# Attention feeding a mixture of experts on one core: two pairs of heads handled as one unit, with the tail keys in 64x64 quarters of the array

## The chip, the cores and the metric

The kernel runs on one core of a Trainium2 chip. The metric is the device time of one execution in microseconds (us), the median of several executions. The engines of the core are named as in the profile: PE is TensorE (matmuls), PEld its weight loads, DVE is VectorE, ACT is ScalarE, POOL is GpSimd, and SP is SyncE, which here only issues transfers (DMAs). Each engine runs its own instructions in order and waits for others by semaphores.

## The reference

An attention with a soft cap on the scores feeds a mixture of experts in which each token goes to one expert.

```python
batch, n_heads, seq, head_dim = (8, 12, 448, 64)            # cap = 30
scores = q @ k.T / sqrt(head_dim)
scores = cap * tanh(scores / cap)
attn = exp(scores - scores.max(-1)); attn /= attn.sum(-1) + 1e-9
x = (attn @ v) as [3584 tokens, 768]                        # 12 heads x 64
logits = x @ w_gate + modality_bias[modality_id]            # 8 experts
e_idx, gate_w = argmax(logits), softmax(logits)[e_idx]
out[token] = gate_w * (relu(x[token] @ w1[e]) @ w2[e])      # F = 1024
```

## The kernel before, in words

**Two phases.** `attention` works on 48 pairs of heads (six per batch, eight batches; a pair is heads 2p and 2p+1 of one batch). Then `run_slots` works on blocks of 384 tokens of one expert (slots): `ffn1` (tokens times w1), `ffn2` (times w2). In slot 0 some work that is left over from attention is put between the matmuls of `ffn1` by hooks.

**Scores.** The scores of a pair stand as [keys, queries]. The raw keys and queries of a pair (tile `raw`, 128 partitions: 64 dimensions of the one head, 64 of the other) are split by `prep` into two float32r halves, `ah` (high) and `al` (low); a product is three float32r matmuls (high x high, low x high, high x low). A head has 448 keys: three steps of 128 keys (`scores` with step 0, 1, 2) and 64 keys that are left, the tail. In steps 0 to 2 the two heads' matmuls are two at a time, in the upper and the lower 64 rows of the array, each into a bank of a `sc` tile. In step 3 the tails of both heads are one matmul of 128 rows: the 128 tail keys stand in a block with zeros beside them, so that each key meets its own head only.

**Weights.** ACT makes Tanh (`th`) and Exp (`pt`, or `sh` for step 3) from each `sc` tile. There are two `sc` buffers; a Tanh sets its buffer free.

**Sums over keys.** `weigh_own` multiplies the exponentials with `va` (the values) in plain float32, six matmuls, the two heads side by side in the two halves of the array's columns; `weigh_shared` adds the tails with one matmul of 128 rows and 128 columns. The result `xT` [dimension, query] is copied to SBUF by DVE (L603). DVE also adds the three exponential tiles of a head (`add`, L472 and L473, into `tot`).

**Denominators and gate logits.** `sums` works on three pairs at a time: each pair has 32 columns of the array and the same 32 partitions of the bank `glog`; four float32 matmuls per pair accumulate two sums of exponentials and 16 gate logits. `by_token` transposes the result to tokens (`lt`), `logits` divides, `rows_out` transposes `xT` to token rows (four transposes into `tp`) and multiplies by the reciprocal (`xs`), `store` writes them to DRAM.

**Order.** The order on PE is written out by hand (instructions are pinned), over g = 0 to 48, four steps each; the weighing of pair g-1 stands between the scores of pair g. After the last pair of a batch `route` finds each token's expert, in stages; its second PE piece is the small matmul pair `rank`. When seven batches are routed, `early_slot` names the expert of slot 0, whose w1 is loaded and split (`split_w`) and whose tokens are gathered while attention ends; `transpose` turns the gathered rows into `x`.

**Slot 0.** `run_slot` splits `W2_EARLY` of the eight w2 tiles on POOL ahead of `ffn1`, the other tiles behind it, and then loads the next slot's w1:

```python
if n == TW:
    self.load_w2(cur[0], raws, range(W2_EARLY if between else FC), self.nc.gpsimd if between else None)
self.ffn1(n, between)
if between:
    self.load_w2(cur[0], raws, range(W2_EARLY, FC))
    nxt = ahead()
```

The loads of w1 and w2 share four `raw` buffers. In `ffn2` ACT takes each finished half tile out of PSUM (`ot<-py`, two `py` buffers).

## Time and profile before

| | us |
|---|---|
| median of 3 runs (lowest, highest) | 939.42 (939.24, 940.53) |
| the profiled execution, its own time | 939.73 |
| its span, from the first to the last instruction | 938.1 |

The profiled execution spent 1.6 us outside its span. In rows of the trace, a start is counted from the beginning of the span; a busy time of a matmul includes the drain of the array, so that consecutive matmuls overlap, and what a matmul costs in a stream is the distance from its start to the next start. A plain float32 matmul is recorded as two (`x12` for six of them).

### The profile page before, as it was taken

What the parts mean: (1) busy time and instruction counts of PE and PEld (TensorE: products, weight loads), DVE (VectorE), ACT (ScalarE), POOL (GpSimd) and SP (SyncE); (2) the same over time, 40 slices, a digit from 0 to 9 for tenths busy, and PEclk for the clock granted to TensorE, in tenths of its full rate; (3) what the DMA queues carried; (4) which work ended last, traced back from release to release, by engine and by line L of the source; (5) the groups of instructions that cost most, each with busy time, mean ns of one, the idle gap of its engine ahead of it and who ended that gap; (6) DMA issues with size and microseconds to landing.
All of it is one profiled execution on the core that took longest, in us unless ns stands there. A gap on an engine that the chain in (4) does not pass through costs nothing. (4 is left out here: it accounts for less than half of the span.)

```text
span 938.1 us, 14512 instructions
## 1 busy us (share of the span) xinstructions
PE 902.5 (96%) x5360; PEld 699.3 (75%) x5360; DVE 545.9 (58%) x939; ACT 557.6 (59%) x758; POOL 138.8 (15%) x147
## 2 busy tenths in 40 slices
PE   7999999999999998989899999999999999999997
PEld 3444545554545554469899999999999999998997
DVE  4667777778787777567444443433434444427762
ACT  5998888888888886732434444343424444435551
POOL 2000202020202022124310202020201102020000
PEclk8999999999999999999999999999999999999997
DMA  4333434444534533642764735353554646247660
GB/s 143 111 104 120 125 127 127 126 110 144 127 127 103 151 108 93 233 141 71 264 225 129 235 125 201 116 178 129 168 203 146 225 130 206 93 133 258 197 211 7
DMA packets 47467, 140.01 MB, mean 149 GB/s; under 512 B 8687, under 2 KB 9631, under 8 KB 47377
## 3 DMA queue, kind: packets, MB, share of 16 engines
q1 hardware_dynamic: 38464, 106.47, 36.9%
q0 software_dynamic: 8768, 32.42, 10.0%
q8 instruction: 47, 0.77, 0.3%
q14 instruction: 44, 0.35, 0.1%
q10 hardware_dynamic: 144, 0.00, 0.0%
HBM read 117.35 MB, written 22.69 MB: 149 GB/s over the span
## 5 line engine op out<-in xcount | busy, mean ns | idle before, releaser
L460 ACT ACTIVATE th<-sc,isc 128x896 f32<-128x896 f32 x192 | 168.6, 907 | 53.4 <-PE sc L458 53.2
L775 PE MATMUL ph<-x,al 128*128 128x384 f32 (+2 forms) x528 | 167.8, 318 | 0.0
L800 PE MATMUL py<-bh,hh 128*128 128x384 f32 x464 | 159.5, 344 | 5.6 <-ACT ot L805 4.1
L800 PE MATMUL py<-bh,hl 128*128 128x384 f32 x464 | 157.2, 339 | 0.0
L800 PE MATMUL py<-bl,hh 128*128 128x384 f32 x464 | 156.8, 339 | 0.0
L462 ACT ACTIVATE pt<-th,cabs 128x896 f32<-128x896 f32 x144 | 149.5, 1044 | 3.1 <-DVE tot L473 0.4
L771 PE MATMUL ph<-x,ah 128*128 128x384 f32 x384 | 129.8, 338 | 4.7 <-DVE x L754 4.4
L467 PE MATMUL xT<-pt,va 128*64 128x448 f32 x576 | 122.8, 563 | 8.7 <-DVE xT L603 7.1
L772 PE MATMUL ph<-x,ah 128*128 128x384 f32 x384 | 129.2, 336 | 0.0
L727 DVE TENSOR_TENSOR bl<-raw,bh 128x768 fp32r<-128x768 f32 x85 | 78.6, 955 | 52.1 <-ACT bh L726 49.6
L726 ACT CAST bh<-raw 128x768 fp32r<-128x768 f32 x88 | 70.2, 840 | 63.0 <-DMA raw<-in_w_dram 52.6
L775 PEld LDWEIGHTS ph<-x,al 128*128 128x128 f32 x528 | 102.0, 193 | 0.0
L458 PEld LDWEIGHTS sc<-ah 64*128 64x128 f32 (+1 forms) x336 | 36.5, 187 | 77.8 <-ACT pt L462 28.5
L781 ACT ACTIVATE hh<-ph 128x384 fp32r<-128x384 f32 x64 | 30.6, 489 | 105.6 <-PE ph L775 98.4
L805 ACT ACTIVATE ot<-py,mt 128x384 f32<-128x384 f32 x58 | 33.6, 581 | 99.2 <-issue 50.1
L800 PEld LDWEIGHTS py<-bh,hh 128*128 128x128 f32 x464 | 87.5, 189 | 6.5 <-ACT ot L805 4.4
L810 POOL DMA_INDIRECT out_dram<-ot,mt x29 | 33.0, 1137 | 391.0 <-ACT ot L805 310.4
L467 PEld LDWEIGHTS xT<-pt,va 128*64 128x64 f32 x576 | 38.1, 139 | 70.6 <-issue 46.5
L458 PE MATMUL sc<-ah 64*128 64x448 f32 (+1 forms) x336 | 86.8, 445 | 3.0 <-ACT th L460 2.0
L727 DVE TENSOR_TENSOR al<-raw,ah 128x1024 fp32r<-128x1024 f32 x64 | 76.4, 1222 | 22.1 <-ACT ah L726 21.9
L800 PEld LDWEIGHTS py<-bl,hh 128*128 128x128 f32 x464 | 87.6, 189 | 0.3 <-DVE bl L727 0.2
L800 PEld LDWEIGHTS py<-bh,hl 128*128 128x128 f32 x464 | 87.6, 189 | 0.1
(165 smaller groups left out, 1352.3 us busy)
## 6 DMA issues: line engine op xcount, KB each, us to landing
raw<-in_w_dram SPq DMA_DIRECT2D x88, 384.0 KB
raw<-in_w_dram SPq DMA_DIRECT2D x64, 512.0 KB
raw<-in_kq_dram SPq DMA_DIRECT2D x47, 480.0 KB
va<-in_v_dram SPq DMA_DIRECT2D x48, 256.0 KB
xd<-xs POOLq DMA_DIRECT2D x15, 672.0 KB
kq<-in_w_dram SPq DMA_DIRECT2D x2, 512.0 KB
xd<-xs SPq DMA_DIRECT2D x1, 672.0 KB
mapd<-pay,pos POOLq DMA_INDIRECT x32
```

The lines of the kernel that those rows point to most:

```text
L458: pin(pe.matmul(sc[:, j, :S], k[rows, ks], q[rows, KC2:], start=i == 0, stop=i == 2))
L460: nc.scalar.activation(th[:, :n], sc[:, :n, :S], AF.Tanh, scale=self.isc)
L462: nc.scalar.activation(dst, th[:, :n] if step < KU else th[:, 0], AF.Exp, scale=self.cabs)
L467: pin(pe.matmul(xT[j * D : (j + 1) * D, :S], va[:, u * D : (u + 1) * D], pt[:, u], start=u < 2, stop=False))
L726: keep((self.nc.vector.tensor_copy if busy else self.nc.scalar.copy)(hi, raw))
L727: (keep if minus is None else (lambda inst: inst))((minus or self.nc.vector).tensor_tensor(lo, raw, hi, op=ALU.subtract))
L771: nc.tensor.matmul(ph[:, :w], hi[:, fs], self.x[:, k, 0, :w], start=first, stop=False)
L772: nc.tensor.matmul(ph[:, :w], hi[:, fs], self.x[:, k, 1, :w], start=False, stop=False)
L775: nc.tensor.matmul(ph[:, :w], lo[:, fs], self.x[:, k, 0, :w], start=False, stop=last)
L800: nc.tensor.matmul(py[:, :HALF], self.h[a][:, f, rows], self.w2s[f][c][:, cs], start=i == 0, stop=i == 3 * FC - 1,)
L805: nc.scalar.mul(ot[:, cs], py[:, :HALF], mt[:, t, 1:2])
L810: nc.gpsimd.indirect_dma_start(self.out, bass.IndirectOffsetOnAxis(ap=mt.bitcast(I32)[:, t, 0:1], axis=0), ot, None, bounds_check=NT - 1, ...
```

## The change

Two pairs of heads (the even pair A = 2d and the odd pair G = 2d+1 of the same batch) form one unit d, 24 in all.

- **Tail keys.** No zeros are loaded any more: `raw` has 384 own keys, 448 queries and 64 tail keys per head. The tail scores are taken from `raw` itself, in plain float32: four matmuls of 64 rows and 64 columns (`scores_left`), pair by columns, head by rows. One Tanh and one Exp of 896 columns per unit replace two of each of 448 columns. `prep` splits 832 columns in place of 960. The tails' part of the weighing is again four float32 matmuls in quarters (`weigh_left`), pair by rows, head by columns.
- **Copies and rows.** `xT` is two banks wide and copied once per unit; the rows of both pairs are transposed eight at a time into an `sc` buffer and multiplied by one instruction (L561). The store has 256 columns per unit in place of 384 per three pairs.
- **Sums.** Four groups of 32 columns per unit, two matmuls each; transposition, reciprocal and logits once per unit.
- **Order.** Written out anew, by units. The first w1 tiles go into the ring of key and query buffers as these come free; two of the six tiles are cast and subtracted on POOL. `W2_EARLY` is 4 in place of 3.

The core of the diff:

```diff
-W2_EARLY = 3
+W2_EARLY = 4
-            def scores(step, pt, sh, hi, lo):
...
-                n = 2 if step < KU else 1
...
-                        rows = slice(j * D, (j + 1) * D) if step < KU else slice(0, 128)
-                        pin(pe.matmul(sc[:, j, :S], k[rows, ks], q[rows, KC2:], start=i == 0, stop=i == 2))
+            def scores_left(d):
+                shs[d] = xp.tile([128, 2, S], F32, name="sh", bufs=2)
+                sc = ps_s.tile([128, 2, 512], F32, name="sc")
+                for i in range(2):
+                    raw = ring[(2 * d + i) % RING]
+                    for j in range(2):
+                        rows = slice(j * D, (j + 1) * D)
+                        pin(pe.matmul(
+                            sc[i * KR : (i + 1) * KR, j, :S], raw[rows, QL:QK], raw[rows, OWN:QL], start=True, stop=True
+                        ))
+                weights(shs[d], sc)
-            def weigh_shared(xT, sh, va):
-                pin(pe.matmul(xT[:, :S], va[:, 2 * KU * D :], sh, start=False, stop=True))
+            def weigh_left(xT, d):
+                for i in range(2):
+                    rows = slice(i * KR, (i + 1) * KR)
+                    for j in range(2):
+                        o = (2 * KU + j) * D
+                        pin(pe.matmul(
+                            xT[j * D : (j + 1) * D, i, :S], vas[2 * d + i][rows, o : o + D], shs[d][rows, j],
+                            start=False, stop=True,
+                        ))
+                xs_ = kept[d] = xp.tile([128, 2, S], F32, name="xT", bufs=2)
+                pin(V.tensor_copy(xs_, xT[:, :, :S]))
...
-                for t in range(HB):
-                    xs_, tot, sh = kept[h * HB + t]
-                    w = self.pick[:, part] if part < 3 else self.wgt[:, (h * HB + t) % NP]
-                    rhs = (tot[:, 0], tot[:, 1], sh, xs_)[part]
-                    pin(pe.matmul(self.glog[t * GW : (t + 1) * GW, :S], w, rhs, start=part == 0, stop=part == 3))
+                group = lambda x: glog[x * GW : (x + 1) * GW, :S]
+                for i in range(2):
+                    for j in range(2):
+                        pin(pe.matmul(group(2 * i + j), self.pick[:, 0], tots[2 * d + i][:, j], start=True, stop=False))
+                for j in range(2):
+                    pin(pe.matmul(group(j), self.pick[:, 1], shs[d][:, j], start=False, stop=True))
+                for i in range(2):
+                    pin(pe.matmul(
+                        group(2 + i), self.wgt[:, (2 * d + i) % NP], kept[d][:, i], start=False, stop=True
+                    ))
+            for d in range(ND):
+                A, G = 2 * d, 2 * d + 1
+                early, end = d == SOON + 2, d == ND - 1
...
+                scores(A, 0)
+                scores(A, 1)
...
+                if d:
+                    xT = ps_x.tile([128, 2, 512], F32, name="xT")
+                    weigh_own(xT, A - 2)
+                    add(A - 2)
...
+                prep(A + 2)
...
+                scores(A, 2)
+                scores(G, 0)
...
+                if d:
+                    weigh_own(xT, A - 1)
+                    add(A - 1)
...
+                prep(A + 3)
...
+                scores(G, 1)
+                scores(G, 2)
+                if not end:
+                    scores_left(d)
...
+                if d:
+                    weigh_left(xT, d - 1)
...
+                go_on()
+                if d >= 2:
+                    if not early:
+                        logits(d - 2)
+                    tokens(d - 2, nc.sync if early else nc.gpsimd)
...
+                if d:
+                    sums(d - 1)
+                    copy_sums()
```

The first place is PE in the middle of attention. Before, one pair reads, from its weighing (`xT<-pt,va`) on: the sums of three pairs (`glog`), step 2, step 3 (the tails: one matmul in place of two), the transposes of an older pair and the tails' weighing.

```order
L467 MATMUL xT<-pt,va 64x448 x6
L486 MATMUL glog<-tot,pick 32x448 x6
L458 MATMUL sc<-ah_157 128x448 x2
L458 MATMUL sc<-ah_157,al_158 128x448 x2
L458 MATMUL sc<-al_158,ah_157 128x448 x2
L458 MATMUL sc<-ah_157 128x448
L458 MATMUL sc<-ah_157,al_158 128x448
L458 MATMUL sc<-al_158,ah_157 128x448
L516 MATMUL tp<-ident,xT 112x128 x4
L476 MATMUL xT<-sh,va 128x448
```

After the change, the end of a unit on PE: step 2 of the odd pair, then the tails of both pairs and everything that is done once per unit, up to the first scores of the next unit.

```order
L461 MATMUL sc<-ah_158 128x448 x2
L461 MATMUL sc<-ah_158,al_159 128x448 x2
L461 MATMUL sc<-al_159,ah_158 128x448 x2
L472 MATMUL sc<-raw 64x448 x4
L490 MATMUL xT<-sh,va 64x448 x4
L525 MATMUL lt<-ident,gl 112x128 x4
L553 MATMUL tp<-ident,xT 112x128 x8
L509 MATMUL glog<-tot,pick 32x448 x4
L511 MATMUL glog<-sh,pick 32x448 x2
L513 MATMUL glog<-xT,wgt 32x448 x2
L461 MATMUL sc<-ah_152 128x448 x2
```

The tails' scores and everything behind them, up to the next unit's scores, now stand in one run at the unit's end. Before, scores stood between them.

The second place is ACT in slot 0, behind `ffn1`: the casts of the last w2 tiles (`bh`), those of the next slot's w1 (`ah`), and the emptying of the finished `py` tiles (`ot`). Before:

```order
L726 CAST bh_4429<-raw 128x768
L726 CAST bh_4431<-raw 128x768
L726 CAST bh_4433<-raw 128x768
L726 CAST bh_4435<-raw 128x768
L726 CAST bh_4437<-raw 128x768
L726 CAST ah_149<-raw 128x1024
L805 ACTIVATE ot<-py,mt 128x384 x2
```

And after the change:

```order
L770 CAST bh_4320<-raw 128x768
L770 CAST bh_4322<-raw 128x768
L770 CAST bh_4324<-raw 128x768
L770 CAST bh_4326<-raw 128x768
L849 ACTIVATE ot<-py,mt 128x384
L770 CAST ah_148<-raw 128x1024
L770 CAST ah_150<-raw 128x1024
L849 ACTIVATE ot<-py,mt 128x384
```

Four w2 tiles are cast here in place of five, and the first `ot` stands ahead of the next slot's first w1 cast.

## Rows read from the trace of the kernel before

**Rows 1.** The page: the span, and the busy time of each engine with its share and its instructions.

```profile
span 938.1 us, 14512 instructions
PE 902.5 (96%) x5360; PEld 699.3 (75%) x5360; DVE 545.9 (58%) x939; ACT 557.6 (59%) x758; POOL 138.8 (15%) x147
```

**Rows 2.** Busy time by stretch: the stretch and its length, then busy time (and instructions) of PE, PEld, DVE, ACT and POOL, the granted clock as a share, the DMA share and GB/s. The first stretch is the middle of attention; the second goes from the first scores after the seventh batch to the first matmul of `ffn1`; the third is `ffn1` of slot 0, the fourth the beginning of its `ffn2`.

```profile
100.00:150.00 50.00, 49.30 (x309) 25.50 (x309) 38.21 (x73) 43.62 (x52) 7.44 (x8) 1.00 0.42 119
...
358.17:404.84 46.67, 37.19 (x216) 18.64 (x216) 34.64 (x73) 33.37 (x42) 10.28 (x10) 0.96 0.59 176
404.84:438.73 33.89, 33.77 (x200) 30.16 (x200) 21.38 (x88) 5.87 (x11) 11.91 (x11) 0.95 0.30 88
438.73:459.00 20.27, 16.18 (x85) 15.32 (x85) 10.34 (x11) 10.73 (x15) 11.06 (x13) 0.92 0.78 259
```

**Rows 3.** PE in order of time in the middle of attention: start, busy time, line, operation, tiles, array rows*columns, shape, count. One pair goes from 205.04 to 213.30.

```profile
205.04 2.48 PE L467 MATMUL xT<-pt,va 128*64 128x448 f32 x12
207.44 1.70 PE L486 MATMUL glog<-tot,pick 128*32 128x448 f32 x12
209.08 0.47 PE L458 MATMUL sc<-ah 64*128 64x448 f32 x2
...
209.89 0.47 PE L458 MATMUL sc<-ah 128*128 128x448 f32 x1
...
210.60 0.60 PE L516 MATMUL tp<-ident,xT 128*112 128x128 f32 x4
211.04 0.92 PE L476 MATMUL xT<-sh,va 128*128 128x448 f32 x2
211.89 0.47 PE L458 MATMUL sc<-ah 64*128 64x448 f32 x2
...
212.80 0.37 PE L458 MATMUL sc<-ah,al 64*128 64x448 f32 x2
213.00 0.37 PE L458 MATMUL sc<-al,ah 64*128 64x448 f32 x2
213.30 2.48 PE L467 MATMUL xT<-pt,va 128*64 128x448 f32 x12
...
219.31 0.92 PE L476 MATMUL xT<-sh,va 128*128 128x448 f32 x2
220.06 0.49 PE L498 MATMUL lt<-ident,gl 96*112 96x96 f32 x4
220.49 0.47 PE L458 MATMUL sc<-ah 64*128 64x448 f32 x2
```

**Rows 4.** PE in order of time: the first scores of all, the first scores of pair 4 and those of pair 44 (40 pairs later).

```profile
7.86 0.74 PE L458 MATMUL sc<-ah 64*128 64x448 f32 x2 [0.94 <-DVE ah L446]
...
37.58 0.47 PE L458 MATMUL sc<-ah 64*128 64x448 f32 x2
...
358.17 0.47 PE L458 MATMUL sc<-ah 64*128 64x448 f32 x2
```

**Rows 5.** ACT in order of time in the middle of attention; in brackets the idle time before, and what ended it.

```profile
228.63 1.00 ACT L460 ACTIVATE th<-sc,isc 128x896 f32<-128x896 f32 x1
229.66 1.04 ACT L462 ACTIVATE pt<-th,cabs 128x896 f32<-128x896 f32 x1
230.61 0.99 ACT L460 ACTIVATE th<-sc,isc 128x896 f32<-128x896 f32 x1
...
242.54 1.53 ACT L460 ACTIVATE th<-sc,isc 128x896 f32<-128x896 f32 x2 [1.32 <-PE sc L458]
```

**Rows 6.** The costliest groups of DVE between 60 and 300 us: line, engine, operation, tiles, shapes, count, busy time in all, mean ns of one, idle time before and what ended it.

```profile
L447 DVE TENSOR_TENSOR al<-raw,ah 128x960 fp32r<-128x960 f32 x30 | 34.7, 1158 | 0.9
L473 DVE TENSOR_TENSOR tot<-tot,pt 128x896 f32<-128x896 f32 x30 | 32.8, 1093 | 2.6
...
L517 DVE TENSOR_TENSOR xs<-tp,rec 112x512 f32<-112x512 f32 x31 | 21.4, 690 | 38.9 <-PE tp L516 36.0 <-PE sc L458 2.9
...
L446 DVE CAST ah<-raw 128x960 fp32r<-128x960 f32 x30 | 19.5, 651 | 0.0
...
L603 DVE COPY xT<-xT 128x448 f32<-128x448 f32 x31 | 19.3, 623 | 1.3
```

**Rows 7.** PE in order of time around the three longest waits between attention and slot 1, the second with the next matmuls, and two matmuls of `ffn1` that stand 24 apart.

```profile
370.29 4.17 PE L467 MATMUL xT<-pt,va 128*64 128x448 f32 x12 [2.57 <-DVE xT L603]
...
404.84 0.69 PE L771 MATMUL ph<-x,ah 128*128 128x384 f32 x1 [4.43 <-DVE x L754]
405.32 0.52 PE L772 MATMUL ph<-x,ah 128*128 128x384 f32 x1
405.64 0.52 PE L775 MATMUL ph<-x,al 128*128 128x384 f32 x1
...
429.88 0.33 PE L771 MATMUL ph<-x,ah 128*128 128x384 f32 x1
...
434.04 0.33 PE L771 MATMUL ph<-x,ah 128*128 128x384 f32 x1
...
451.62 0.44 PE L800 MATMUL py<-bh,hh 128*128 128x384 f32 x1 [4.08 <-ACT ot L805]
```

**Rows 8.** ACT at the last of these waits: the cast of the next slot's first w1 tile waits for its transfer, the two `ot` stand behind it.

```profile
450.04 1.04 ACT L726 CAST ah<-raw 128x1024 fp32r<-128x1024 f32 x1 [5.11 <-DMA raw<-in_w_dram]
450.99 1.05 ACT L805 ACTIVATE ot<-py,mt 128x384 f32<-128x384 f32 x2
```

More of the change, by code (lines that the diff above doesn't have):

```diff
@@ L238, in route @@
         yield
-        rank = ps.tile([128, 512], F32, name="rank", tag="small")
+        rank = bank()[:, S:] if bank else ps.tile([128, 512], F32, name="rank", tag="small")
         rk = rank[:CP, : C * E]
@@ new lines, in prep, with weights @@
+                for cs in (slice(0, QL),) if g else (slice(0, OWN), slice(OWN, QL)):
+                    pin((nc.scalar.copy if cs.start else V.tensor_copy)(hi[:, cs], raw[:, cs]))
+                    pin(V.tensor_tensor(lo[:, cs], raw[:, cs], hi[:, cs], op=ALU.subtract))
+            def weights(dst, sc):
+                th = pp.tile([128, 2, S], F32, name="th")
+                nc.scalar.activation(th, sc[:, :, :S], AF.Tanh, scale=self.isc)
+                nc.scalar.activation(dst, th, AF.Exp, scale=self.cabs)
@@ L459, in scores @@
-                th = pp.tile([128, 2, S], F32, name="th")
-                nc.scalar.activation(th[:, :n], sc[:, :n, :S], AF.Tanh, scale=self.isc)
-                dst = pt[:, 2 * step : 2 * step + 2] if step < KU else sh
-                nc.scalar.activation(dst, th[:, :n] if step < KU else th[:, 0], AF.Exp, scale=self.cabs)
-            def weigh_own(xT, pt, va):
+                    for j in range(2):
+                        rows = slice(j * D, (j + 1) * D)
+                        pin(pe.matmul(sc[:, j, :S], k[rows, ks], q[rows, OWN:], start=i == 0, stop=i == 2))
@@ L540, in attention, with go_on, load_w1, split @@
+            def go_on():
+                for way in routing:
+                    next(way, None)
+            def load_w1(ks):
+                for k in ks:
+                    raws[k] = self.load_raw(self.first_e, self.w1, k, FF, ring[k])
+            def split(k, cast, minus):
+                self.split_w(raws[k], self.w1s[k], pin=True, cast=cast, minus=minus)
+            SOON = (B - 1) * NP // 2 - 1
+            raws = {}
             self.warm(self.ps_r, 4)
-            kqs, vas = {}, {}
@@ L635, in attention @@
-            for pair in adds:
-                add(*pair)
-            self.raws = [self.load_raw(e, self.w2, k, DM) for k in range(self.nstage)]
-            def tokens(h):
-                xs = xp.tile([CP, C, HB * 128], F32, name="xs", bufs=2)
-                for t in range(HB):
-                    rows_out(h, t, xs, recs[h], self.ps_t, "ptr")
-                store(h, xs)
-            def last_sums():
-                for part in range(4):
-                    sums(NH * B - 1, part, self.ps_y, "py")
-                self.last_gl = copy_sums()
+            fetch_kq(2)
@@ new lines, in move @@
+            def move(k):
+                self.transpose(k, *((self.ps_r, "small") if k % 3 == 2 else (ps_s, "sc")), pin=True)
+            xT = ps_x.tile([128, 2, 512], F32, name="xT")
+            weigh_own(xT, G - 1)
+            split(4, None, V)
+            for k in range(4):
+                move(k)
+            add(G - 1)
+            split(5, None, nc.gpsimd)
+            weigh_own(xT, G)
+            for k in range(4, KC):
+                move(k)
+            weigh_left(xT, ND - 1)
+            add(G)
@@ L651, in last_logits, with before_last @@
+            self.raws = [self.load_raw(self.first_e, self.w2, k, DM) for k in range(self.nstage)]
+            def before_last():
+                logits(ND - 2)
+                tokens(ND - 2, banks=lambda: self.ps_t.tile([128, 512], F32, name="tp", tag="ptr"))
+                sums(ND - 1, self.ps_y, "py")
+                copy_sums()
             def last_logits():
-                recs[NH * B - 1] = logits(NH * B - 1, by_token(self.last_gl), lgs[B - 1])
+                logits(ND - 1)
                 self.way = self.route(B - 1, lgs[B - 1], rp, self.ps_r)
@@ L1048, in layout @@
             va[..., o : o + D] = vp[:, :, j, i * 128 : (i + 1) * 128]
-        rows, o = slice(j * KR, (j + 1) * KR), (2 * KU + j) * D
-        va[:, :, rows, o : o + D] = vp[:, :, j, last]
+        o = (2 * KU + j) * D
+        for i in range(2):
+            va[:, i::2, i * KR : (i + 1) * KR, o : o + D] = vp[:, i::2, j, last]
     wg = np.asarray(inputs["moe_w_gate"])
```

328 lines of the change are left out of this document (149 added, 179 removed).

## The prediction

> **What bounds the kernel now.** First the page: PE is busy for 96% of the span, DVE and ACT for 58% and 59% [rows 1]. A busy matmul can hide waits, so I read next, by stretches, where PE is not full. In the middle of attention it works 49.30 of 50 us at the full granted clock, with ACT at 43.62 and DVE at 38.21 [rows 2]: PE bounds attention, but ACT has only 13% to spare. From the first scores of pair 44 to the first matmul of `ffn1` PE works 37.19 of 46.67 us, and at the beginning of `ffn2` of slot 0 16.18 of 20.27 [rows 2]. From pair 4 to pair 44 the kernel goes 358.17 - 37.58 = 320.6 us for 40 pairs, 8.015 each or **16.03 for two** [rows 4].
>
> What a pair is made of, from start to start [rows 3]: weighing 2.40, sums 1.64 (205.04 to 207.44 to 209.08), step 2 0.81, tails' scores 0.71, four transposes 0.44, tails' weighing 0.85, steps 0 and 1 1.41 (211.89 to 213.30). A matmul pair in float32r costs 0.20 (212.80 to 213.00); a plain float32 matmul of 448 columns costs 0.75 where the array keeps its shape (219.31 to 220.06). A new shape costs about 0.1 on either side: step 2 takes 0.81 behind the sums, where three pairs of 0.20 are 0.60.
>
> **What the change does to a unit on PE.** Own scores and weighing stay: three times two steps at 1.42, twice 2.41, together 9.08. New behind them:
> - Tails' scores: four quarters, 0.75 if they run together, plus 0.16 for the new shape: 0.91. Before, 2 x 0.71.
> - Tails' weighing: 0.78 in the same shape. Before, 2 x 0.75 to 0.85.
> - Transposes to logits 0.44 (from 0.43, 220.06 to 220.49; once per unit, before once per three pairs), eight row transposes 0.92 (from 2 x 0.44).
> - Sums: two rounds of four groups, 1.64. Before, twelve matmuls for three pairs in two halves of 1.64, that is 2.19 for two pairs.
>
> The run at the unit's end is 0.91 + 0.78 + 0.44 + 0.92 + 1.64 = 4.69, and PE's work 13.8 per unit. The trace has no quarter in float32 and no four column groups. Nearest are rows with two or three neighbours: the two heads side by side in the weighing, six matmuls in 2.40, that is 0.80 per two, and the sums' three groups, 1.64 for two rounds, both as fast as a lone one of 0.75 plus the new shape [rows 3]. So I take "together", 0.75; the other end is one after another, 3.0. A gain below 0.75 is excluded, since each streams its 448 columns as a lone one does.
>
> The Trainium skill speaks against this: "TensorE: Matmul & The Clock Gate", Part 3, lists packed matmuls at 3.07 times a lone one's rate for four and 2.38 for three, so four would take 4/3.07 = 1.30 lone ones. Three would take 1.26 by it; the trace's rounds of three, 0.82 with the new shape in it, are against that. By the page a round of four would take about 0.98 here, an estimate, and the sum would be about 925.
>
> **Why the whole gain does not come.** ACT does seven steps per unit. A step of Tanh and Exp takes 1.98 (228.63 to 230.61) [rows 5], so 13.9 per unit; before, six such and two short ones, about the same. PE's 13.8 and ACT's 13.9 cannot overlap fully, as there are two `sc` buffers and the run of 4.69 gives ACT nothing after the tails' scores. I walk one unit: even step 0 is done at 0.71, its Tanh starts 0.21 later (as at 213.00 + 0.20 of work, and Tanh at +0.4, in all steps that ACT waits for). Four ACT steps bring 0.92 + 7.92 = 8.84; the Tanh of the odd pair's step 1 frees the buffer for the tails' scores 1.03 + 0.06 later, at 9.93. PE was ready at 9.08 and has waited **0.85**. Behind this wait stands the whole run, and behind that the next unit's scores, for which ACT waits. With the run of 4.69 the next unit starts at **14.6**. ACT idles about 0.9 there, as now before each pair (1.32) [rows 5].
>
> DVE is hidden: two adds 2.17 per pair, cast and subtraction scaled to 832 columns 0.56 + 1.00 per pair, the wide copy 0.62 + 448 x 1.05 ns = 1.09, the wide row multiply 0.69 + 512 x 1.05 ns = 1.23 (1.05 ns per column, from 690 and 623 ns for 512 and 448 columns) [rows 6], with the copy of the sums 0.6 and small ones 0.9, 11.3, plus some 3.5 of routing in each third unit: at most 14.8 there. If that cover goes, the next scores wait for the row multiply. In a routing unit the tails wait 0.38 longer, as ACT has the routing's Exp too, and `rank` takes 0.25: 15.25. The mean is 14.83, so **16.03 - 14.83 = 1.20 less per unit, over units 2 to 21 24.0 us**. Units 0 and 1 are set by ACT at either version (their start at 7.86 and the seven steps are the same): 0. POOL's and SP's issues (24 stores in place of 16, key loads of 448 KB in place of 480) come units ahead of their use: 0.
>
> **Between attention and slot 1.**
> - *Units 22, 23 up to `ffn1`*, now 46.67 [rows 2], with 2.57 and 4.43 of waiting and a weighing mostly at the clock's lower level, 1.2 GHz (4.17 [rows 7] in place of 2.48 [rows 3]). I walk them with the same durations. In unit 22 DVE does the routing of the seventh batch ahead of the adds: it is through with it at 6.2, with adds, splits and `early_slot` (2.4) at 16.0, with the wide copy at 17.0, and the last sums, which wait for that copy, end at 17.8. In unit 23 the tails' scores stand first (18.7); ACT's seven steps of 1.98 run on to 32.8. PE weighs pair 46 until 34.3, transposes four tiles of `x` (1.4, with 0.9 of waiting for DVE), weighs pair 47 (2.4), does two more tiles (0.7) and the tails (0.8): 40.9. With 1 us for a stretch at the low clock, **42.0: 4.7 less**. The gather has until 34.3 for this; what it comes later, it adds.
> - *`ffn1` of slot 0*, now 33.89: 144 matmuls at 0.173 (24 from 429.88 to 434.04) are 25.0, some nine of them at the low clock 0.32 instead (405.32 to 405.64) [rows 7], 1.3, and 7.6 is attention's rest. After: 25.0 and 1.64 + 2 x 0.44 + 2 x 0.92 + rank and shapes 0.8 = 5.2: **3.7 less**.
> - *`ffn2` of slot 0*: PE waits 4.08 because the two `ot` stand behind a cast that waits 5.11 for its transfer [rows 7, 8], and then the clock falls: a mean of 0.92 over 20.27 us [rows 2] is 3.2 us at half speed, 1.6 lost. After, the first `ot` stands ahead of that cast and there is one w2 tile less to load before it. PE can then do a third half tile (24 x 0.176 = 4.2) before it needs the second `ot`, which stands behind two casts. Between 0 and 5.7 I take 4.5, as 4.2 covers the 4.08: **4.5 less**.
>
> **Sum**: 24.0 + 4.7 + 3.7 + 4.5 = 36.9. From the profiled execution's own 939.73 (span 938.1 and 1.6 around it; 0.3 above the median) that is **903**.
>
> **Rivals.**
> 1. *A round of four is a third slower than a lone matmul*: a third of the way from together (0.75) to two after two (1.5), 1.0. Tails' scores, weighing and two rounds of sums stand in the run, where nothing hides them: 4 x 0.25 x 24 = 24, so 927. Against it: rounds of two and three show none of it [rows 3]. 0.08. It is about what the Trainium skill's table for packed matmuls (the page and part above) would give.
> 2. *DVE becomes late.* The wide multiply has five dimensions from two banks; if it takes twice as long, 2.4, or the adds stretch beside it, the next unit's second scores wait for their buffer by about 0.9: 22 units, 923. For: DVE goes from 38.21/50 = 76% [rows 2] to 12.3/14.8 = 83% busy. Against: in the walk DVE is idle for 3.3 us ahead of the wide copy in plain units. 0.12.
> 3. *Quarters run two at a time*: tails' scores and weighing 0.75 longer each, 1.5 x 24 = 36: 939 less 2, as `ffn1` then waits less for its `x`: 937, nearly as before. For: pairs by rows and pairs by columns are in the trace, both at once are not. 0.05.
> 4. *Quarters run one after another* (slower than before): 2.25 longer each, 4.5 x 24 = 108, less what ACT then no longer waits for: about 1005. It decides from 36.9/24 = 1.54 on: if the two quarter groups together take over 3.2 us in place of 1.69, the kernel is slower. Against: no pair in the trace runs so. 0.05.
>
> **Numbers.** The forecast has 0.70, its own range 893 (no waits in routing units, nothing lost in `ffn2`, no low clock) to 915 (12 us of late gather, low clock and DVE delays). With rivals 1 and 2 in it, the range is 893 to 927 and leaves out about 1 in 8. A change of 0.2% is what a measurement of this kernel can tell from none. Faster: 0.70 + 0.08 + 0.12 and a little of rival 3, held to 0.91; same 0.03; slower 0.06.
>
> **What would show it.** The middle of attention: distance from unit to unit 14.6, and 15.2 in each third; the first tails' matmul waits about 0.85 for ACT's Tanh; from it to the tails' weighing 0.91, from there to the logits' transposes 0.78; sums 1.64. If these two are near 1.6 or 3.0, rivals 3 or 4 hold. ACT over 90% busy, no PE wait for DVE but at `rank`. `ffn1` begins near 375. Wrong it would be made by a PE wait for the row multiply in each unit, by a gather that lands after 368, or by a wait for `ot` in slot 0 that stays above 3 us.

## The result: 27 us faster, where 37 were forecast

The changed kernel takes **913.13 us** (median of 4 runs, 912.3 to 913.79) against 939.97 for the kernel before on the same chip; the ratio is 0.9714 with a 95% interval of [0.9697, 0.9731]. The profiled execution took 913.67 with a span of 912.1.

The page of the changed kernel, busy time and share as in [rows 1]:

```profile
span 912.1 us, 14765 instructions
PE 862.0 (95%) x5536; PEld 674.4 (74%) x5536; DVE 538.5 (59%) x966; ACT 548.6 (60%) x709; POOL 159.0 (17%) x161
```

Busy time by stretch, with the columns of [rows 2]: the middle of attention, units 22 and 23 up to the first matmul of `ffn1`, `ffn1` of slot 0, `ffn2` of slot 0:

```profile
100.00:150.00 50.00, 46.74 (x355) 22.82 (x349) 37.99 (x70) 46.14 (x50) 9.68 (x11) 1.00 0.39 124
330.08:380.97 50.89, 40.52 (x266) 18.59 (x262) 36.87 (x71) 31.72 (x37) 21.59 (x16) 0.90 0.53 149
380.97:411.18 30.21, 30.10 (x187) 28.07 (x188) 20.63 (x93) 6.59 (x12) 13.67 (x12) 1.00 0.34 94
411.18:442.53 31.35, 28.71 (x163) 27.93 (x163) 16.92 (x20) 17.39 (x26) 14.58 (x17) 0.95 0.68 229
```

In attention PE is no longer full (46.74 of 50, before 49.30) and ACT is at 46.14. The second row holds the surprise: the stretch that was to shrink from 46.67 to 42.0 has grown to 50.89, at a mean clock of 0.90. Against the terms of the prediction, each stretch as after minus before:

| stretch | forecast | measured | from |
|---|---|---|---|
| up to unit 2 (pair 4) | 0 | -2.3 | 35.26 - 37.58 |
| units 2 to 21 | -24.0 | -25.8 | 294.82 - 320.59, a unit 14.74 in place of 16.03 |
| units 22, 23 | -4.7 | **+4.2** | 50.89 - 46.67 |
| `ffn1` of slot 0 | -3.7 | -3.7 | 30.21 - 33.89 |
| `ffn2` of slot 0 | -4.5 | **-1.6** | 31.35 - 32.96 (438.73 to 471.69 before) |
| from slot 1 on | 0 | +3.2 | 469.57 - 466.41 |
| sum (span) | -36.9 | -26.0 | 912.1 - 938.1 |

What PE waits for, in all, times and longest; above, the two largest of the changed kernel, below, the same wait for the gather in the kernel before:

```profile
PE sc L472 <- ACT th L448: 17.5, 22, 0.9
PE ptr L788 <- DMA xg<-xd,mt: 10.0, 5, 3.5
```

```profile
PE ptr L744 <- DMA xg<-xd,mt: 0.5, 1, 0.5
```

The first is the forecast wait of the tails' scores for ACT. The second was not in the sum: 10.0 us in which PE stands before the transposes of `x` and the gathered rows (`xg`) have not landed, 7.4 of it for slot 0 and 2.6 for slot 1.

**The middle of attention.** PE in order of time, the run at the end of one unit, with the next unit's first scores:

```profile
192.56 0.98 PE L472 MATMUL sc<-kq 64*64 64x448 f32 x8 [0.78 <-ACT th L448]
193.37 0.93 PE L490 MATMUL xT<-sh,va 64*64 64x448 f32 x8
194.23 0.65 PE L525 MATMUL lt<-ident,gl 128*112 128x128 f32 x4
194.71 1.04 PE L553 MATMUL tp<-ident,xT 128*112 128x128 f32 x8
195.68 0.96 PE L509 MATMUL glog<-tot,pick 128*32 128x448 f32 x8
...
197.32 0.47 PE L461 MATMUL sc<-ah 64*128 64x448 f32 x2
```

Start to start: tails' scores 0.81 (forecast 0.91), tails' weighing 0.86 (0.78), logits' transposes 0.48 (0.44), row transposes 0.97 (0.92), sums 1.64 (1.64). The run is 4.76 where 4.69 was forecast, and the wait ahead of it 0.78 where 0.85 was. Four quarters of the array work side by side.

**Between attention and slot 1.** PE in order of time in unit 23, from the weighing of pair 46 to the first matmul of `ffn1`:

```profile
362.39 2.48 PE L480 MATMUL xT<-pt,va 128*64 128x448 f32 x12
367.76 0.25 PE L788 MATMUL ptr<-identr,xg 128*128 128x128 f32 x1 [2.90 <-DMA xg<-xd,mt]
371.50 0.37 PE L788 MATMUL ptr<-identr,xg 128*128 128x128 f32 x1 [3.48 <-DMA xg<-xd,mt]
372.85 1.13 PE L788 MATMUL ptr<-identr,xg 128*128 128x128 f32 x7 [0.98 <-DMA xg<-xd,mt]
374.38 0.62 PE L788 MATMUL ptr<-identr,xg 128*128 128x128 f32 x3 [0.40 <-DVE x L798]
374.93 4.41 PE L480 MATMUL xT<-pt,va 128*64 128x448 f32 x12
...
380.97 0.41 PE L815 MATMUL ph<-x,ah 128*128 128x384 f32 x1
```

PE is through with pair 46 at 364.9, 34.8 after unit 22 began (forecast 34.3). The three tiles of the gather come at 367.8, 371.5 and 372.8. Then, after 7.4 us of idling, pair 47 is weighed in 4.41 in place of 2.48: from 374.93 to 379.27 the granted clock is 0.55, nearly all of it at the 1.2 GHz level. 10.1 us in place of 2.3 up to that weighing, and 1.9 in place of 1.0 for the low clock, are 8.7 of the 8.9 between +4.2 and -4.7.

Why is the gather late? POOL issues the whole chain: scatter of the map of rows (`mapd`, four), load of the map (`mt`), three gathers. POOL before and after, in order of time:

```profile
364.03 1.28 POOL L267 DMA_INDIRECT mapd<-pay,pos  x1 [5.38 <-DVE epair L300]
...
375.98 0.60 POOL L701 DMA_DIRECT2D mt<-mapd  x1 [5.06 <-DMA mapd<-pay,pos]
385.33 1.05 POOL L708 DMA_INDIRECT xg<-xd,mt  x1 [8.58 <-DMA xd<-xs]
...
387.99 1.00 POOL L708 DMA_INDIRECT xg<-xd,mt  x1 [0.30 <-issue]
```

```profile
341.53 0.99 POOL L267 DMA_INDIRECT mapd<-pay,pos  x1 [10.17 <-DVE epair L300]
...
345.87 0.94 POOL L267 DMA_INDIRECT mapd<-pay,pos  x1 [0.30 <-issue]
357.15 0.74 POOL L745 DMA_DIRECT2D mt<-mapd  x1 [10.34 <-DMA mapd<-pay,pos]
...
359.12 3.28 POOL L771 TENSOR_TENSOR al<-kq,ah 128x1024 fp32r<-128x1024 f32 x1
362.57 2.22 POOL L752 DMA_INDIRECT xg<-xd,mt  x1 [0.16 <-issue]
...
366.41 1.23 POOL L752 DMA_INDIRECT xg<-xd,mt  x1 [0.30 <-issue]
```

From the first scatter to the first gather is 21.3 before and 21.0 after, but that is not the same chain twice. Before, the load of the map was issued 12.0 after the first scatter, and then the gather stood 8.58 for the store of the rows (`xd<-xs`), which had been issued only at 377.63. After, the load of the map is issued 15.6 after the first scatter, and the store has landed (at 360.8) before the gather could start. From the first gather to the third landed tile is 8.5 before and 10.3 after. In all, first scatter to third tile, that is 29.8 before and 31.3 after: the scatter and the gathers take longer, and a wait for the store has gone.

What changed more is where the chain stands. It starts 11.5 into unit 22 (341.53 - 330.08) where it started 5.9 after the scores of pair 44 (364.03 - 358.17), and PE now comes to the transposes 23.3 after the first scatter, where it came 29 after it (393.0) before. What was just hidden before (PE waited 0.46 for the third tile) lies open now; PE in the kernel before:

```profile
393.83 0.28 PE L744 MATMUL ptr<-identr,xg 128*128 128x128 f32 x1 [0.46 <-DMA xg<-xd,mt]
```

### The profile page after: what moved, and what is told of

Its sections match the earlier page's. It is cut to its first block, busy times and chain, and to the rows that moved or that the text cites. A ratio compares the mean times of both kernels' runs of the same rounds, so it can differ in the third digit from the quotient of the medians.

```text
span 912.1 us, 14765 instructions
## 1 busy us (share of the span) xinstructions
PE 862.0 (95%) x5536; PEld 674.4 (74%) x5536; DVE 538.5 (59%) x966; ACT 548.6 (60%) x709; POOL 159.0 (17%) x161
## 5 line engine op out<-in xcount | busy, mean ns | idle before, releaser
L448 ACT ACTIVATE th<-sc,isc 128x896 f32<-128x896 f32 x168 | 164.1, 994 | 29.7 <-PE sc L461 26.3
L798 DVE TENSOR_TENSOR x<-ptr,x 128x384 fp32r<-128x384 f32 (+2 forms) x66 | 32.6, 517 | 96.6 <-ACT x L797 96.6
L826 DVE SCALAR_TENSOR_TENSOR hl<-ph,hh 128x384 fp32r<-128x384 f32 x64 | 34.8, 555 | 86.0 <-ACT hh L825 85.8
```

Source lines behind the costliest of these rows:

```text
L448: nc.scalar.activation(th, sc[:, :, :S], AF.Tanh, scale=self.isc)
L798: keep(nc.vector.tensor_tensor(lo, pt[:, :w], hi, op=ALU.subtract))
L826: nc.vector.scalar_tensor_tensor(hl[:, f, :w], acc, 0.0, hh[:, f, :w], op0=ALU.max, op1=ALU.subtract)
```

## Experiments

Each is the changed kernel with one edit, unless it says more; times are read against the kernel before, which ran beside each group (medians 937.1 to 940.1), so ratios are to be compared with 0.9714. "Began" gives the first matmul of `ffn1` against the first scores of unit 22 (50.89 in the changed kernel).

**1. The gathers ahead of POOL's split.**

```diff
+                    self.gather(maps, known=NT - S)
                     split(0, nc.gpsimd, nc.gpsimd)
-                    self.gather(maps, known=NT - S)
```

> The changed kernel with the three indirect gathers of slot 0 issued on POOL ahead of the split of the first w1 tile instead of behind it. In the changed kernel POOL issues the row map's load at 357.15, casts and subtracts until 362.4 and issues the gathers at 362.57, 365.10 and 366.41; PE waits 2.90, 3.48 and 0.98 for them, 7.4 in all. Theory A (the gather is late because of what the transfers before it wait for): the row map itself lands 4.9 after 357.15, at 362.0, and the store of the rows, issued at 347.98, lands 12.8 later at 360.8, so the gather moves by at most 0.6 and the time by -0.6 to 0, 912.5 to 913. Theory B (the split on POOL holds it): the split's 4.4 go, the gather is issued near 358 and the time is about 4 less, 909.

Measured: 911.88, ratio 0.9715 [0.9679, 0.9752]; `ffn1` at 380.91. POOL:

```profile
356.45 0.73 POOL L745 DMA_DIRECT2D mt<-mapd  x1 [9.65 <-DMA mapd<-pay,pos]
361.82 2.31 POOL L752 DMA_INDIRECT xg<-xd,mt  x1 [4.48 <-DMA mt<-mapd]
```

With nothing in front of it the gather waits for its map's load until 361.82. Theory A; the split stood in time that the load takes anyway.

**2. and 3. The order of SP's loads in unit 22.** In the second run the store of the rows goes ahead of w1 tiles 2 and 3 and the v tiles; in the third all four w1 tiles go behind it.

```diff
-                if early:
-                    load_w1((2, 3))
...
-                if early:
-                    fetch_v(A + 2)
-                    fetch_v(G + 2)
...
                     tokens(d - 2, nc.sync if early else nc.gpsimd)
+                    if early:
+                        load_w1((2, 3))
+                        fetch_v(A + 2)
+                        fetch_v(G + 2)
```

> The changed kernel with SP's queue in unit 22 put in another order: the store of the rows, and only then the loads of w1 tiles 2 and 3 and of the two v tiles (1.5 MB), which now stand ahead of it. Tiles 0 and 1 stay ahead. Theory A, queue (the scatter of the map and the store wait behind 2.5 MB of loads): the scatter's wait of 10.34 on POOL falls by what 1.5 MB take, some 4 us, the gather is issued 4 earlier, near 358.5, and PE's 7.4 of waiting fall to about 3; 909. Theory B, contention (the gather's and the scatter's own packets share the engines with whatever is loaded, in any order): the gather lands where it did, and the time stays within 1 of 913.

> As the run before, with all four w1 tiles that unit 22 loads put behind the store of the rows. Nothing but the key and value loads of the loop is then in the engines while the map is scattered (341.5 to 346.8). Theory A, queue: the scatter lands about 5 after its last issue, as it does elsewhere in the run (median 5.0 from issue to landing), near 352; the map is loaded by 354.5, the store has landed by then, the gather is issued near 358 behind POOL's split, which now waits for its tile, and PE waits less than 2 of 7.4; 907 to 909, with up to 2 given back where DVE splits w1 tile 2 later and the sums wait. Theory B, contention: the four tiles now collide with the gather instead of the scatter, and the gain is under 2; 911 to 913.

Measured: 911.0, ratio 0.9691 [0.965, 0.9731], and 909.2, 0.9685 [0.965, 0.9721]. Neither is told from the changed kernel by its time; the traces say more. In the second run POOL still waits 10.51 for the scatter. In the third it waits 6.28, but then 6.46 for the load of the map; POOL of the third run:

```profile
353.16 0.62 POOL L743 DMA_DIRECT2D mt<-mapd  x1 [6.28 <-DMA mapd<-pay,pos]
...
360.40 1.05 POOL L750 DMA_INDIRECT xg<-xd,mt  x1 [6.46 <-DMA mt<-mapd]
```

Issues with their median time to landing, of the changed kernel and of the third run, both from 338 to 372:

```profile
mapd<-pay,pos POOLq DMA_INDIRECT x4, 9.8
...
mt<-mapd POOLq DMA_DIRECT2D x1, 3.0 KB, 4.9
```

```profile
mapd<-pay,pos POOLq DMA_INDIRECT x4, 4.0
xg<-xd,mt POOLq DMA_INDIRECT x3, 6.5
mt<-mapd POOLq DMA_DIRECT2D x1, 3.0 KB, 7.0
```

The mechanism is that of theory B: the scatter takes 4.0 with w1 out of its way and 9.8 beside it, and then the next small transfer stands among the loads. For that one, a load of 3 KB, 4.9 and 7.0 are no clean pair, as the DMA engines were busy beside it in both runs (0.98 and 0.88 of the time). "Began" is 48.7 and 48.9, some 2 less, not 4 to 5; but the fourth run, whose program is that of the changed kernel up to there, has 47.5, so that even these 2 are not shown.

**4. Slot 1's transposes one half tile later.**

```diff
-        self.ffn2(cur[1], n, between=moves, wait=2 if raws else 0)
+        self.ffn2(cur[1], n, between=moves, wait=3 if raws else 0)
```

> The changed kernel with the transposes of slot 1's x one half tile (24 matmuls, 4.2) later in ffn2 of slot 0: behind half tiles 3 and 4, three and three, in place of two and two and two behind 2, 3 and 4. In the changed kernel PE waits there 0.41 and 2.23 for slot 1's gather (at 424.56 and 427.07), and eight matmuls behind it take 0.32 in place of 0.175, 1.1 more. Theory A (the gather of slot 1 is what is late next, once the wait for ot is gone): both go, 2.6 + 1.1 = 3.7 less, some 0.5 back for three tiles in a row with two buffers: about 910. Theory B (the gather is late by more than a half tile, or ffn1 of slot 1 then waits for its x): 1 or less gained.

Measured: 909.68, but from 905.5 to 915.5; ratio 0.9703 [0.9647, 0.976]. `ffn2` of slot 0 takes 31.16 in place of 31.35. The wait for the gather is gone, as theory A had it, and in its place PE waits 0.86 for `ot` and 1.36 for `x`. The size is that of theory B (1 or less), the reason neither's.

**5. Half of the sums ahead of the tails' scores.** `sums` is cut after its first round (`sums_own`).

```diff
+                ahead = 0 < d < ND - 1 and d % 3 != 2
+                if ahead:
+                    sums_own(d - 1)
                 if not end:
                     scores_left(d)
...
-                    sums(d - 1)
+                    sums(d - 1, own=not ahead)
```

> The changed kernel with the first round of the sums (four column groups from the added weights, 0.78 on PE) put ahead of the tails' scores instead of at the unit's end, in the units that have no rank (two of three); the others stay as they are and serve as control. Theory A (the loop of the prediction: PE waits 0.78 for ACT at the tails' scores, and the run behind them leaves ACT idle): the round fills the wait, the run is shorter by it, and such a unit takes 13.9 to 14.1 in place of 14.68 to 14.79; 14 units, some 10 less, 903. The control units stay at 14.7. Theory B (ACT alone sets the unit, by its seven steps and pauses that have nothing to do with the run): no unit changes by more than 0.1; 913.

Measured: 905.48, ratio 0.966 [0.9593, 0.9728]. From tails' scores to tails' scores, units with the edit take 14.41 and 14.53 (14.67 and 14.79 in the changed kernel), the control units 14.82 (14.78). Read from first scores to first scores, the same three units take 13.95, 14.42 and 15.38 (14.67, 14.68 and 14.89): the first of them is as short as theory A had it, and the control unit gives 0.49 back, so that it is no control. By either reading three units are some 0.49 shorter, about a third of what theory A had for them. PE in one of these units:

```profile
195.04 0.48 PE L461 MATMUL sc<-ah 64*128 64x448 f32 x2
...
196.12 0.47 PE L461 MATMUL sc<-ah 64*128 64x448 f32 x2 [0.19 <-DVE xs L568]
```

In this unit the wait for ACT is gone; now the unit's second scores wait for the row multiply, which frees their buffer (195.04 to 196.12, where 0.71 was). This is the wait of the prediction's rival 2, called up by a shorter run and not by a late DVE. 14 units by 0.26 are 3.6; the other 2.5 by which `ffn1` is earlier (374.87 in place of 380.97) lie in unit 22, where PE waits 2.88 for DVE's adds ahead of the first round and then less for the gather.

**6. The tails' scores twice.**

```diff
-                for i in range(2):
+                for i in (0, 1, 0, 1):
                     raw = ring[(2 * d + i) % RING]
```

> The changed kernel with the four quarters of the tails' scores issued twice into the same bank, so that a second round stands behind the first in the same shape. Theory A (four quarters together cost what one alone does, and the run counts fully): from the first tails' matmul to the tails' weighing 0.80 becomes 1.55, a unit 14.74 becomes 15.4 to 15.5, 22 units, 16 more, 929. Rival 1 of the prediction (a round of four is a third slower): 1.8 between the two, and 21 more, 934. Theory B (ACT alone sets the unit): PE's extra 0.75 is hidden; 913 to 915.

Measured: 922.63, ratio 0.9851 [0.9781, 0.9922]. PE:

```profile
200.31 1.73 PE L472 MATMUL sc<-kq 64*64 64x448 f32 x16 [0.78 <-ACT th L448]
201.86 0.93 PE L490 MATMUL xT<-sh,va 64*64 64x448 f32 x8
```

1.55 in place of 0.81: a second round of four quarters costs 0.74, what a lone float32 matmul costs in [rows 3] (0.75). Units take 15.38, 15.49 and 15.47 to 15.56, 0.70 more: what is added to the run counts nearly in full, as theory A has it, with the same wait of 0.78 ahead. Of 22 x 0.70 = 15.4 some 12.5 reach `ffn1` (393.45): the gather waits give 3 back.

**7. PE's other work ahead of the transposes.**

```diff
             weigh_own(xT, G - 1)
             split(4, None, V)
-            for k in range(4):
-                move(k)
+            logits(ND - 2)
+            tokens(ND - 2)
             add(G - 1)
             split(5, None, nc.gpsimd)
             weigh_own(xT, G)
-            for k in range(4, KC):
-                move(k)
             weigh_left(xT, ND - 1)
+            for k in range(KC):
+                move(k)
...
             def before_last():
-                logits(ND - 2)
-                tokens(ND - 2, banks=lambda: self.ps_t.tile([128, 512], F32, name="tp", tag="ptr"))
```

> The changed kernel with PE's order behind the weighing of pair 46 changed: logits and row transposes of unit 22 (1.5, which ffn1 has in the changed kernel), the weighing of pair 47 and the tails' weighing (3.3) come first, then all six tiles of x; before, four tiles stood ahead of this work and PE waited 7.4 for the gather in front of them with it at hand. Theory A (the transition was lost to that wait alone): the gather lands near 372.8 as before, PE reaches it at 369.7 instead of 364.9, six tiles take some 3.5, ffn1 begins near 376.5 in place of 381.0 and is 1.5 shorter, and pair 47 is weighed at the full clock: 6 to 7 less, 906. Theory B (DVE sets the start of ffn1 there, with splits, adds, copies and the row multiply, some 12 of work from 365 on): 378 or later, under 4 less in all.

Measured: 910.54, ratio 0.9714 [0.9647, 0.9781]: no gain. `ffn1` begins at 376.76, as theory A expected (376.5). But:

```profile
376.76:385.00 8.24, 8.24 (x43) 6.77 (x44) 3.59 (x5) 3.42 (x5) 4.82 (x3) 0.78 0.30 88
```

`ffn1` now starts behind a stretch of waiting and transposes at the low clock (0.78 over its first 8.2 us), it takes 30.79 in place of the 28.7 that were due, and in `ffn2` PE waits 2.07 and 1.18 for slot 1's gather. Of the 4.2 won at `ffn1` 2.8 are left where slot 1 begins (439.72 in place of 442.53), and the time can't tell them from nothing.

**8. Three early w2 tiles.**

```diff
-W2_EARLY = 4
+W2_EARLY = 3
```

> The changed kernel with three w2 tiles in place of four in the early set, as in the kernel before. The prediction put the end of the wait for ot in ffn2 of slot 0 (4.08) down to this fourth tile, as one tile less stands ahead of the first w1 cast, together with the order of ot and cast on ACT. Theory A (the fourth tile does it): a wait for ot of 2 to 4 comes back and ffn2 of slot 0 grows from 31.35 to 33 to 35; 915 to 917. Theory B (the transfers of slot 1's w1 simply come earlier relative to ffn2, with three or four): no wait over 1, 913.

Measured: 910.03, ratio 0.972 [0.9651, 0.9789]. A wait of 1.64 for `ot` comes back and the wait for slot 1's gather goes; `ffn2` takes 30.08. Between the theories, by one trace of each: with the fourth tile the wait for `ot` is gone, and PE comes so early that it waits for the gather instead.

**9. to 11. Further along the same lines.** The ninth run moves the logits' transposes ahead too, in all units to 21 (in the units with `rank`, that also); the tenth adds the third run's loads and the counts one block earlier; the eleventh adds the seventh run's order.

```diff
+                if d >= 2 and not early:
+                    logits(d - 2)
+                if ahead:
+                    if d % 3 == 2:
+                        go_on()
+                    sums_own(d - 1)
...
-                        self.run_slots(early, (*hooks, (4, order)))
+                        self.run_slots(early, (*hooks, (3, order)))
```

> The changed kernel with both the logits' transposes and the first round of the sums ahead of the tails' scores, in units 1 to 21 (in the units that have rank, it goes ahead too). The run with the first round alone ahead took 14.41 to 14.53 per unit in place of 14.68 to 14.79, not the 13.9 to 14.1 that was expected, and in it the second scores of the next unit wait for the row multiply that frees their buffer. Theory A (that buffer is what took the rest): with the logits out of the run the row transposes come 0.5 earlier, the buffer is free in time, and a unit is bounded by PE's own work, 14.1 to 14.2, and ACT's 13.9; 14.2 to 14.3 in all units, 9 to 11 less than the changed kernel, 902 to 904. Theory B (DVE as a whole is full, with some 12.3 of work and 3.5 more in the units with routing): the units with routing stay at 14.7 to 14.8 and the mean falls by no more than 0.3; 907.

> The run before, with two edits on the chains of transfers: the w1 loads of unit 22 behind the store of the rows, and the counts that start the last plan (and with it slot 1's map and gather) one block of ffn1 earlier, behind block 3 instead of 4 (3.1). Theory A (slot 1's gather is late by its chain, which starts at the counts): its wait of 2.64 in ffn2 of slot 0 falls to under 0.5 and the low clock behind it (1.1) goes; with the 2 of the loads, 5 less than the run before. Theory B (the chain ends with the scatter of the map and the transfers, and the counts are not what it waits for): the wait stays above 1.5, and only the loads' 2 are gained.

> The run before, and PE's order behind the weighing of pair 46 as in the run that filled the wait (logits and rows of unit 22, weighing of pair 47 and the tails ahead of all tiles of x). In that run ffn1 began 4 earlier but ran its first 12 matmuls at the lower clock level, and slot 1's gather took 3.3 back. Theory A (with the chain earlier nothing takes it back): 2 to 4 less than the run before, 892 to 896. Theory B (ffn1 begins earlier, but slot 1's gather stands where it stood, since its chain starts with the last logits in ffn1): within 1 of the run before.

Measured: 917.28, ratio 0.9783 [0.9758, 0.9808]; 919.92, 0.9806 [0.9778, 0.9835]; 921.8, 0.9841 [0.9807, 0.9876]. All three are slower than the changed kernel. Two units of three take 14.38 with no wait of PE at all: cut up, PE's work is itself 14.38, where such a unit had 14.68 - 0.78 = 13.90 with the run in one piece. Every third takes 16.59. There DVE, with the logits in hand early, does the routing ahead of the copy of the weighed rows (`xT`) that the sums need:

```profile
255.45 0.88 DVE L211 TENSOR_REDUCE L<-lg 112x32 f32<-112x384 f32 x1
...
258.74 1.08 DVE L495 COPY xT<-xT 128x896 f32<-128x896 f32 x1
```

```profile
259.88 0.95 PE L520 MATMUL glog<-xT,wgt 128*32 128x448 f32 x4 [1.11 <-DVE xT L495]
```

Of the 2.21 by which this unit is longer, 1.11 is this wait and 0.66 is the round behind it, whose two halves now run one after the other; the rest lies at `rank`. Neither theory said that; theory B had DVE, but as full, not as busy with the wrong thing first. In the tenth run the wait for slot 1's gather is gone, as theory A had it, and a wait of 3.55 for `x` stands in its place: `ffn2` of slot 0 33.56. In the eleventh PE waits 4.84 for DVE's `x` before `ffn1`. What remains of their expectations can't be read off, as the loop was lost.

**12. The chain first.** The fifth run's loop (but not in unit 22), and in unit 22 DVE's adds and split behind rank and positions.

```diff
+                if d and not early:
                     add(A - 2)
...
-                prep(A + 2)
                 if not early:
+                    prep(A + 2)
                     go_on()
...
                     load_w1((0, 1))
+                    add(A - 2)
+                    prep(A + 2)
```

> The changed kernel with the first round of the sums ahead of the tails' scores in units 1 to 21 that have no rank, and in unit 22 one more edit: DVE's adds of pair 42 and the split of the next keys (3.8) stand behind rank, positions and counts of the seventh batch instead of ahead of them. In the changed kernel they ran from 336.40 to 339.03 and 339.15 to 340.18, between the routing and its positions, and POOL issued the first scatter at 341.53, 11.45 after the unit's start. Theory A (ffn1 of slot 0 begins when the chain of scatter, map and gather is through, whatever PE did before): the chain starts 2.5 earlier in its unit, near 9, and ffn1 begins 2.5 earlier against the unit's start, near 48.4 in place of 50.9; with 13 units shorter by 0.26, 3.4, the time is 906 to 908. Theory B (the transfers set it: w1's loads move forward with the chain and collide with it as before): the first scatter is earlier, but the gather lands where it did against the unit's start, and only the loop's 3.4 are gained, 909 to 910.

Measured: **903.18**, ratio 0.9653 [0.9611, 0.9694], the lowest of all, 3.5% below the kernel before. Its interval lies just below the changed kernel's, but within the fifth run's, so the time does not tell the new edit from the loop alone. Unit 22 begins at 327.12:

```profile
335.69 0.99 POOL L267 DMA_INDIRECT mapd<-pay,pos  x1 [6.55 <-DVE esc L299]
...
356.39 1.08 POOL L765 DMA_INDIRECT xg<-xd,mt  x1 [0.69 <-DMA mt<-mapd]
```

The first scatter comes 8.6 into the unit in place of 11.5, the first gather 29.3 in place of 32.5, and the last tile 37.6 in place of 42.8; PE waits 1.96 for it in place of 7.4, and `ffn1` begins at 45.4 in place of 50.9. In the traces that is theory A: what starts the chain earlier starts `ffn1` earlier, though `w1` moves along with it. That it gains more than the 2.5 expected is not shown, as the fifth run has 48.4 there and the fourth 47.5 with the chain as it was.

## Why the prediction was right, and which step was wrong

**Right in direction, and by its own mechanism in the loop.** The four quarters run together (0.81 and 0.86 against 0.91 and 0.78 forecast; a further round 0.74). Rivals 1, 3 and 4 fall with that. The table of the Trainium skill ("TensorE: Matmul & The Clock Gate", Part 3), with 3.07 for four, had given an estimate of 0.98 for a round; here the measurement decides. The wait for ACT ahead of the run is 0.78 (0.85 forecast), a plain unit takes 14.68 (14.6), and a routing unit 14.89 where 15.25 was forecast, as the tails wait only 0.90 there and not 1.23: a mean of 14.74 against 14.83, which is the 1.8 beyond the forecast 24.0. Rival 2 did not come in the changed kernel: PE waits for DVE nowhere in units 2 to 21. Runs 5 and 9 show how near it was.

The total was also helped: 1.8 more in the loop and 2.3 in units 0 and 1 were not in the sum. Without these 4.1 the time would have been about 917, above the 915 that the forecast itself allowed.

**The step that failed** is the transition: "The gather has until 34.3 for this; what it comes later, it adds." That sentence named the cause and put no price on it. The gather's last tile came at 42.8 (372.85 - 330.08), which is 8.5 late, and the stretch missed its forecast by 8.9. (The walk's terms behind 34.3 also add up to 40.5, not to the 40.9 written there.) A price was to be had from the trace of before: first scatter 364.03, third tile at 393.83, so 29.8 from one to the other. Laid against the walk, with the scatter behind DVE's routing, adds and splits, some 10 into the unit (an estimate), it gives 39.8, some 5 late. It is a price seen afterwards and a rough one, as 8.58 of it was a wait for the store of the rows. The rest is a scatter that came at 11.5, and a chain of 31.3 in place of 29.8: the load of the map now follows the first scatter by 15.6 and not 12.0, as the scatter stands beside w1's loads (runs 2 and 3), and the gathers take 10.3 and not 8.5. The prediction did name 368 as the time from which this would make it wrong, and held 12 us for it in the range; the forecast itself should have had some 5 of them.

**The same step a second time** is `ffn2` of slot 0, -1.6 for -4.5. The wait for `ot`, 4.08, went, as said, and run 8 shows that the fourth early tile is part of why. But what PE would meet next was not asked: slot 1's gather, 0.41 + 2.23. That leaves 1.4 of the 4.08, and the clock, from which 1.6 were to come back, has the same mean over the stretch as before, 0.95 (the row of before stands below). Runs 4, 8 and 10 each take the wait for the gather away, and each time another appears, for `ot` or `x`; in run 7 it grows. The stretch stays within 30.1 and 33.6.

```profile
438.73:471.69 32.96, 28.88 (x163) 27.93 (x163) 17.85 (x21) 18.21 (x27) 15.47 (x17) 0.95 0.70 230
```

**Other terms.** `ffn1` of slot 0 is exact, -3.7. "Units 0 and 1 are set by ACT at either version" was wrong by 2.3 in the kernel's favour: before, the first weighing ran at 1.2 GHz throughout, and ACT waited 2.78 behind it. Mean clock of that weighing before, and of the one that stands there after:

```profile
17.61:22.29 4.68, 4.68 (x15) 1.24 (x13) 0.26 (x1) 2.85 (x3) 0.00 (x0) 0.50 0.00 0
```

```profile
22.48:25.56 3.08, 3.08 (x15) 0.96 (x14) 2.57 (x6) 3.08 (x5) 0.00 (x0) 1.00 0.45 113
```

From slot 1 on the changed kernel is 3.2 longer. Half of it is the end: from the first matmul of the last `ffn2` to the end of the span 16.93 in place of 15.27, and all of that behind the last store's issue (7.4 in place of 5.8). All profiles of kernels with this change show 16.85 to 16.94 there; of the kernel before there is only one, so that the change is not shown to be the cause. Nothing was tried on it, and its cause is open, as is that of the other 1.5.

## What to carry to other kernels

When a change makes the critical engine faster, list the chains that it does not make faster (dependent transfers above all), take their length from the old trace, link by link with what each link waited for, and set each against the new time at which its result is wanted: a chain that was hidden by a hair becomes the bound. A wait that is taken away needs the question "and what does the engine meet next?" answered with a time, not with a reservation. Filling a wait by cutting a run in pieces pays only for what the pieces do not cost: here 0.48 of 0.78 went to the cuts themselves, and a few small instructions put ahead on DVE took more than all of it.

## What the runs showed of the hardware

**Small transfers beside large ones.** A scatter of one row per partition took 4.0 to land (median of four) in run 3, where the DMA engines were 1% busy while it was issued, and 9.8 in the changed kernel beside w1's loads, which are on another queue. The Trainium skill ("DMA: Bandwidth & Descriptors", Queues, rings and completion order) says that each DMA engine alternates between its queues packet by packet. The runs fit an interleaving in that the scatter does not wait for all of the loads; its price beside them was 2.4 times that without.

**DVE and POOL together.** An add of two tiles, 1.09 in the middle of attention, took 3.17 while POOL subtracted; DVE first, then POOL:

```profile
377.14 3.17 DVE L500 TENSOR_TENSOR tot<-tot,pt 128x896 f32<-128x896 f32 x1
```

```profile
376.54 2.81 POOL L771 TENSOR_TENSOR al<-raw,ah 128x1024 fp32r<-128x1024 f32 x1 [4.74 <-ACT ah L770]
```

It ends 0.96 after POOL's. The Trainium skill ("SBUF — State Buffer", Who interferes with whom) has such a DVE instruction, with two inputs in SBUF, contend with a POOL instruction that reads SBUF; the trace agrees, with 2.1 us lost on DVE here. DVE's own subtraction at 357.80 likewise took 2.33 beside POOL's, and 1.23 at 363.87 without. The splits that the change puts on POOL are therefore not free for DVE, though PE shows no wait behind this add.

**The wait for such a chain differs between executions.** The changed kernel and run 4 have the same program up to `ffn2` of slot 0, but in their profiles PE waited 7.4 for the gather in one and 4.0 in the other (0.58, 1.90 and 1.54). A difference of 3 us in this stretch between two single traces proves nothing by itself.
